# A new hand-written order for the first block, and a last product taken by output tile, in a kernel of attention and two MLPs on one core

## The chip, the cores and the metric

The kernel runs on one core of one Trainium2 chip. The metric is the device time of one execution in microseconds (us), and the comparison is with the kernel before the change. The engines that the text names are TensorE (PE, with its weight loads as PEld), VectorE (DVE), ScalarE (ACT), GpSimd (POOL) and the queue of SyncE (SP) that issues most of the DMA transfers.

## What is computed

A chunked attention with eight memory keys is followed by two MLPs over its 3072 rows of 512 numbers. The scale factors of the inputs are left out here.

```python
# q, k, v: 4 batches x 8 heads x 768 x 64; mem_k, mem_v: 4 x 8 x 8 x 64; chunk 32
for c in range(24):
    q_c = q[:, :, 32*c : 32*c + 32]
    k_ctx, v_ctx = k, v of rows max(0, 32*c - 16) .. min(768, 32*c + 40)
    scores = q_c @ concat(mem_k, k_ctx).T / 8
    a = exp(scores - max(scores)); a = a / (sum(a) + 1e-9)
    out[:, :, 32*c : 32*c + 32] = a @ concat(mem_v, v_ctx)
x = out as 3072 rows x 512
h = max(max(x @ w1, x @ w2), x @ w3)        # 512 -> 768
x = h @ w_mid                               # 768 -> 512
h = x @ w_in                                # 512 -> 2048
g = 0 where h <= -1, (h + 1)**2 / 4 between, h where h >= 1
out = g @ w_out                             # 2048 -> 512
```

## The kernel before

**Products.** Each of the four MLP stages keeps its operands as a sum of two rounded numbers, a high and a low part. `mm3` (L544) issues three matmuls for each product: high by high (L545), high by low (L546) and low by high (L547). The weights of the first MLP arrive in chunks of 512 KB (the steps `f`, L124 and L126). Two chunks make a pair, and a pair q is turned into its high and low part in six steps: `wa` (ACT, L139), `wr` (ACT, L143), `wc` (DVE, L147, L148 and L150), `wd` (DVE, L155), `wh` (ACT, L204, the high part) and `ws` (DVE, L209, the low part).

**Blocks.** Rows are taken in blocks of 512, which are four units of 128 rows. Attention is computed unit by unit: loads of k, q and v (`lk`, `lq`, `vs`; `vs` is two transfers of 56 KB), transposes of k and q (`tk` L297, `tq` L328), their copies (`ck`, `ek`, `kw`, `cq`), scores (`s`, L402), the maximum (`mx`, DVE L415 and L416), the exponential (`ex`, ACT L419), the division (`n`, DVE L422, L423 and L425), transposes of the probabilities (`a`, L444), their copy (`ca`), the product with v (`o`, L470), and the high and low part of its result (`cx`, ACT L481, and `dx`, DVE L485).

**The first block.** For block 0 nothing runs ahead that could cover the loads, so the order of its work and of units 0 to 8 is written by hand, as the string `PLAN` (L42 to L58). Its words are the steps above with their number, and the program issues them from left to right. Each engine and the SP queue takes its instructions in this order and waits at its head. A transfer that SP issues also waits for the one eight places ahead of it. `g0` to `g2` are the first products (with w1, w2, w3) over the left 256 of the block's 512 rows, which need units 0 and 1; `l0` to `l2` are the same for the right 256 rows, which need units 2 and 3. From `l3` on a product covers all 512 rows. `gt` and `lt` take the maximum of the three (ACT copy or DVE L582), `lh` splits it, `m` is a product with w_mid. The words `d3` and `d7` are `warm` (L1057): four matmuls of 256 columns on a constant, whose result in bank 3 or 7 nobody reads. A group of them into a bank whose content is still to be read waits for the reader; a group behind `o3` into bank 3 waits for `dx3`.

**The rest.** Behind the plan a list of slots goes through the other blocks and then through the second MLP, in three pairs of blocks. Its last part, `pair_l4`, runs 48 steps for a pair. In each step `l4_mms` (L764) issues three matmuls into the accumulator of each of two output tiles d. At the very end `last_evict` (L930) goes through two halves of 256 rows: DVE adds for both tiles (L937), PE transposes (L939), ACT copies the half (L941) and SP sends it (L943, 256 KB).

Of the kernel before, what the change touches and what calls it, by code (L numbers as in the profile page):

```python
# [39 lines left out]


PLAN = """  # L42
d7 lk1 lmem0 d3 d7 tk1 ck1 mem0 d3 lk0 tk0 lq0 ck0 d3 f0 d3 tq0 d3 ek1 f1 d3 kw0 cq0 wa0 lk2 lm0 s0
lq1 lk3 mx0 lq2 d7 vs0 tk2 vs6 ck2 lk4 d3 wc0 ex0 d3 ek2 tq1 cq1 kw1 wr0 n0 d3 d3 tk3 ck3 f3 d3 s1
ek3 tq2 kw2 d3 d3 d3 mx1 vs5 wd0 ex1 d3 a0 d3 cq2 ca0 s2 wh0 d7 d7 f2 n1 wa1 d7 vs2 lq3 d3 d7 a1 vs1
mx2 d3 mv0 vs3 ex2 lq4 tk4 d7 d3 d7 wr1 ck4 d3 ws0 ek4 tq3 wc1 wd1 kw3 vs7 lk5 mv1 vs4 d3 o0 cq3 f5
f4 cx0 n2 ca1 s3 d7 tq4 wh1 tk5 ck5 mx3 mv2 d3 d3 a2 cq4 dx0 ex3 vs8 d7 vs10 o1 ek5 kw4 d3 ws1 n3
lq5 s4 cx1 wa2 dx1 ca2 vs9 mx4 vs11 wc2 kw5 g0 ex4 d3 vs13 f7 g1 vs12 gt0 gt1 tq5 a3 d7 n4 cq5 vs15
s5 vs14 f6 wr2 wd2 o2 cx2 ca3 f9 vs16 dx2 g2 a4 gt2 wh2 f8 o3 mx5 d7 vs19 ws2 cx3 dx3 ex5 d3 n5 l0
wa3 d3 wr3 lt0 vs18 wc3 vs17 wa4 l1 lt1 l2 wd3 lt2 wr4 ca4 wc4 lq7 l3 f11 lt3 wh3 f10 a5 l4 wd4 o4  # L50
tq7 lh2 wh4 ws3 l5 ws4 wa5 cq7 lk6 cx4 f13 lt4 wc5 l6 d3 f12 wr5 wd5 ca5 lq6 vs23 vs20 lt5 wa6 tk6
lt6 lk7 dx4 wh5 wr6 vs21 vs22 ck6 wc6 tq6 f14 ws5 lk8 l7 tk7 wd6 lh5 lm1 ck7 f15 lt7 ek7 o5 kw6 wh6
cq6 lq8 vs25 cx5 l8 wa7 wr7 ws6 f17 dx5 f16 tk8 s6 l9 mv6 mx6 lt8 lt9 wc7 ck8 m0 wd7 vs27 l10 ek8
wa8 lk9 wc8 f19 ex6 f18 tq8 tk9 wh7 m1 wr8 ws7 wd8 lh8 lt10 kw7 wh8 f21 f20 l11 ws8 ck9 n6 wa9 m2 a6
vs24 wr9 wa10 lk11 lt11 wc9 vs26 wd9 wr10 f23 ca6 l12 l13 cq8 o6 wh9 wc10 ws9 wd10 lt12 s7 lh11 lt13
l14 mx7 cx6 wh10 l15 dx6 f22 vs28 m3 ex7 f24 lt14 f25 ek9 n7 ws10 wa11 vs29 lq9 wc11 wr11 vs30 a7
l16 lt15 kw8 ca7 lh14 vs31 lt16 o7 wd11 cx7 dx7 l17 s8 wh11 lt17 mx8 ws11 ex8 lq10 lh17 lk10
""".split()  # L58
# [10 lines left out]
def attention_then_two_mlps(ctx, tc, q, k, v, mem_k, mem_v, w1, w2, w3, w_mid, w_in, w_out, out):  # L69
    nc = tc.nc  # L70
# [856 lines left out]

    extra, acc4 = [], {}

    def last_evict(p):  # L930

        for i in range(2):
            z = banks[i].rearrange("p (t c) -> p t c", t=2)
            c = slice(i * HK, (i + 1) * HK)
            for d in range(2):
                u2 = fb[4 + d]
                nc.vector.tensor_tensor(out=u2[:, c], in0=acc4[5][d][:, c], in1=u2[:, c], op=ALU.add)  # L937
                for t in range(2):
                    nc.tensor.transpose(z[:, t, d * P:(d + 1) * P], u2[:, (2 * i + t) * P:(2 * i + t + 1) * P], ident)  # L939
            o = fb[i].rearrange("p (t c) -> p t c", t=2)  # L940
            nc.scalar.copy(out=o, in_=z)  # L941
            r0 = 2 * p * TB + 2 * i * P
            nc.sync.dma_start(out=out[r0:r0 + 2 * P, HK:].rearrange("(t p) d -> p t d", p=P), in_=o)  # L943
# [299 lines left out]
```

## Time and profile before

| what | us |
|---|---|
| median of three runs (lowest, highest) | 950.63 (950.12, 950.81) |
| the profiled execution | 953.2 |
| its span in the profile | 951.4 |
| PE busy | 941.1 (99%) |
| DVE busy | 706.7 (74%) |
| ACT busy | 569.5 (60%) |
| POOL busy | 339.3 (36%) |
| DMA share of 16 engines | 53.5% |

PE is at work nearly all the time, in 7154 matmuls. The span is divided by the profile into 40 slices. PE shows 90% or more in all of them but the first and the last, and the row of the granted clock shows 9 in all but one. So the time that is not PE work at full rate lies in the first slices and in the last one, and a reader has to open these two places.

### The profile page before, as it was taken

The page shows a single profiled execution, that of the slowest core. Times are in us where ns is not written, and L with a number is a line of the kernel's source. Part 1 is how long each engine was busy: PE and PEld are TensorE (multiplying, and loading weights), DVE is VectorE, ACT ScalarE, POOL GpSimd, SP SyncE. Part 2 cuts the span into 40 slices and gives each one's busy share as a digit, 9 for nine tenths or more (in the row PEclk, how much of TensorE's full clock was granted, in tenths as well). Part 3 has the DMA queues.
Part 4 walks back from the last instruction along what each step waited for, and adds up shares of the span by engine and source line. Part 5 has one row for each costly group of instructions (what it writes and reads, how often), then busy time and mean ns, then how long its engine had stood idle before and what let it go on. Part 6 is the DMA issues. An engine that isn't in the chain of part 4 may idle for free.

```text
span 951.4 us, 18968 instructions
## 1 busy us (share of the span) xinstructions
PE 941.1 (99%) x7154; PEld 777.7 (82%) x7154; DVE 706.7 (74%) x995; ACT 569.5 (60%) x1037; POOL 339.3 (36%) x331
## 2 busy tenths in 40 slices
PE   8999999999999999999999999999999999999998
PEld 6888888888888888888888888888888888888886
DVE  5989866687887878743347778987777998778854
ACT  6667546554553444333357777677777776777763
POOL 0000002321321111112656654555665555655542
PEclk9989999999999999999999999999999999999999
DMA  9877647677757686433423339524236744233823
GB/s 218 204 197 220 166 115 188 172 232 198 206 155 190 184 199 205 145 110 112 138 84 99 95 97 291 155 39 122 84 91 205 213 112 106 81 91 90 260 67 67
DMA packets 245549, 142.84 MB, mean 150 GB/s; under 512 B 174290, under 2 KB 223186, under 8 KB 245458
## 3 DMA queue, kind: packets, MB, share of 16 engines
q1 hardware_dynamic: 245458, 141.63, 53.5%
q8 instruction: 56, 0.92, 0.4%
q14 instruction: 35, 0.29, 0.1%
HBM read 109.87 MB, written 31.46 MB: 149 GB/s over the span
## 4 chain that ended last, share of the span: by engine, by line
PE 95%; DMA 2%; DVE 1%; SPq 1%; issue 0%; ACT 0%; DVEq 0%
PE psums L545 30%; PE psums L547 30%; PE psums L546 30%; PE psums L463 2%; PE psums L402 2%; DMA kq<-in_k_dram 1%; DMA st<-in_moe_w_dram 1%; PE psums L470 1%; DMA vw<-in_v_dram 1%; PE psums L297 1%; SPq L289 0%; PE psums L1061 0%; PE psums L328 0%; DVE c L155 0%; DVE p L425 0%
## 5 line engine op out<-in xcount | busy, mean ns | idle before, releaser
L545 PE MATMUL psums<-xh,hi 128*128 128x512 f32 (+1 forms) x444 | 173.8, 391 | 0.0
L546 PE MATMUL psums<-xl,hi 128*128 128x512 f32 (+1 forms) x444 | 171.0, 385 | 0.5 <-DVE xl L485 0.5
L564 POOL TENSOR_TENSOR hl_a<-t,hh_a 128x512 fp32r<-128x512 f32 x30 | 40.3, 1343 | 367.4 <-ACT hh_a L562 367.4
L547 PE MATMUL psums<-xh,lo 128*128 128x512 f32 (+1 forms) x444 | 171.0, 385 | 0.0
L858 POOL TENSOR_TENSOR hb<-h,hb 128x512 fp32r<-128x512 f32 x72 | 99.4, 1381 | 92.6 <-PE psums L547 59.9
L850 ACT CAST hb<-h 128x512 fp32r<-128x512 f32 x144 | 88.8, 622 | 48.2 <-PE psums L546 46.5
L582 DVE TENSOR_TENSOR t<-psums,t 128x512 f32<-128x512 f32 (+1 forms) x74 | 49.8, 673 | 71.4 <-PE psums L547 69.4
L545 PEld LDWEIGHTS psums<-xh,hi 128*128 128x128 f32 x444 | 84.1, 189 | 17.2
L546 PEld LDWEIGHTS psums<-xl,hi 128*128 128x128 f32 x444 | 84.2, 190 | 16.5 <-DVE xl L485 0.7
L547 PEld LDWEIGHTS psums<-xh,lo 128*128 128x128 f32 x444 | 84.0, 189 | 16.6
L677 POOL TENSOR_TENSOR hb<-ra,hb 128x256 fp32r<-128x256 f32 x96 | 75.2, 796 | 59.1 <-ACT hb L676 55.9
L742 ACT ACTIVATE psums<-h 128x512 f32<-128x512 f32 x96 | 57.9, 603 | 60.1 <-DVE h L828 24.0
L547 PE MATMUL psums<-t,hb 128*128 128x512 f32 x192 | 74.8, 390 | 0.0
L545 PE MATMUL psums<-t,hb 128*128 128x512 f32 x192 | 74.7, 389 | 0.0
L546 PE MATMUL psums<-t,hb 128*128 128x512 f32 x192 | 74.7, 389 | 0.0
L677 POOL TENSOR_TENSOR hb<-rb,hb 128x256 fp32r<-128x256 f32 x72 | 55.4, 776 | 39.2 <-ACT hb L676 39.2
L856 DVE TENSOR_TENSOR hb<-psums,hb 128x512 fp32r<-128x512 f32 x66 | 44.9, 680 | 24.8 <-PE psums L547 20.1
L743 ACT ACTIVATE psums<-psums 128x512 f32<-128x512 f32 x96 | 55.9, 582 | 3.1
L545 PE MATMUL psums<-hh_a,hi 128*128 128x512 f32 x144 | 57.3, 398 | 0.0
L883 DVE TENSOR_TENSOR h<-h,h 128x1024 f32<-128x1024 f32 (+1 forms) x42 | 56.5, 1368 | 0.0
L547 PE MATMUL psums<-hh_a,lo 128*128 128x512 f32 x144 | 56.2, 390 | 0.0
L546 PE MATMUL psums<-hl_a,hi 128*128 128x512 f32 x144 | 56.1, 389 | 0.0
(151 smaller groups left out, 2269.0 us busy)
## 6 DMA issues: line engine op xcount, KB each, us to landing
ra<-cd SPq DMA_DIRECT2D x24, 512.0 KB
st<-in_moe_w_out_dram SPq DMA_DIRECT2D x22, 512.0 KB
t<-sd SPq DMA_DIRECT2D x21, 512.0 KB
st<-in_moe_w_dram SPq DMA_DIRECT2D x18, 512.0 KB
st<-in_moe_w_in_dram SPq DMA_DIRECT2D x16, 512.0 KB
sd<-st SPq DMA_DIRECT2D x8, 896.0 KB
vw<-in_v_dram SPq DMA_DIRECT2D x59, 112.0 KB
h<-yd SPq DMA_DIRECT2D x12, 512.0 KB
```

Of the source, the lines that this page charges most:

```text
L545: nc.tensor.matmul(out, whi, xhi, start=first, stop=False)
L546: nc.tensor.matmul(out, whi, xlo, start=False, stop=False)
L547: nc.tensor.matmul(out, wlo, xhi, start=False, stop=last)
L564: e.tensor_tensor(out=lo, in0=h, in1=hi.bitcast(F32), op=ALU.subtract)
L582: nc.vector.tensor_tensor(out=t, in0=s, in1=t, op=ALU.max)
L677: nc.gpsimd.tensor_tensor(out=c[:, 1], in0=t, in1=c[:, 0].bitcast(F32), op=ALU.subtract)
L742: nc.scalar.activation(out=a, in_=x, func=AF.Relu, bias=0.5, scale=0.5)
L743: nc.scalar.activation(out=a, in_=a, func=AF.Square)
L850: nc.scalar.copy(out=hi, in_=x)
L856: nc.vector.tensor_tensor(out=lo, in0=y, in1=hi.bitcast(F32), op=ALU.subtract)
L858: nc.gpsimd.tensor_tensor(out=lo, in0=x, in1=hi.bitcast(F32), op=ALU.subtract)
L883: nc.vector.tensor_tensor(out=x, in0=y, in1=z, op=op)
```

## The change

There are two edits.

1. `PLAN` has the same steps in another order, and four more dummy groups (two `d3` and two `d7`): 45 where there were 41.
2. The last two steps of the last pair's product with w_out are held back and done by output tile: both steps for d = 0, then both for d = 1. `last_evict` is called twice. Behind the first tile DVE adds its 512 rows. Behind the second tile PE transposes the first tile, ACT copies it and SP sends it in one transfer (256 KB, in pieces of 512 bytes); then DVE adds the second tile in two halves, PE transposes each, DVE copies the first half (SP sends it, 128 KB) and ACT copies the second half and sends it on its own queue (128 KB).

```diff
 PLAN = """
...
-s5 vs14 f6 wr2 wd2 o2 cx2 ca3 f9 vs16 dx2 g2 a4 gt2 wh2 f8 o3 mx5 d7 vs19 ws2 cx3 dx3 ex5 d3 n5 l0
...
+d3 o1 d7 n3 s4 cx1 d7 ca2 dx1 mx4 vs10 vs13 wa2 wc2 vs12 vs15 d3 lq5 wr2 ex4 vs14 a3 f6 g0 g1 o2 f7
+wd2 gt0 cx2 f8 gt1 wh2 dx2 g2 tq5 ca3 n4 gt2 o3 ws2 kw5 cq5 cx3 wa3 wr3 f9 vs16 dx3 d3 a4 s5 l0 d3
...
-    def l4_mms(acc, w, hi, lo, f):
-        for d in range(2):
+    def l4_mms(acc, w, hi, lo, f, half=range(2)):
+        for d in half:
             r = slice(d * P, (d + 1) * P)
             mm3(acc[d], w[:, 0, r], w[:, 1, r], hi, lo, f == 0, f == HF - 1)
-        hb.extend((hi, lo))
+        if 0 in half:
+            hb.extend((hi, lo))
...
-    def last_evict(p):
+    def last_evict(p, last):
...
+        r0 = 2 * p * TB
+        rows = out[r0:r0 + TB, HK:].rearrange("(t p) d -> p t d", p=P)
+
+        def turn(d, t):
+            nc.tensor.transpose(banks[d][:, t * P:(t + 1) * P], fb[4 + d][:, t * P:(t + 1) * P], ident)
+
+        both_halves = [slice(i * HK, (i + 1) * HK) for i in range(2)]
+
+        def add(d, c):
+            u2 = fb[4 + d][:, c]
+            nc.vector.tensor_tensor(out=u2, in0=acc4[5][d][:, c], in1=u2, op=ALU.add)
+
+        if not last:
+            add(0, slice(0, TB))
+            return
+        for t in range(4):
+            turn(0, t)
+        nc.scalar.copy(out=fb[0], in_=banks[0])
+        nc.sync.dma_start(out=rows[:, :, 0:P], in_=fb[0].rearrange("p (t d) -> p t d", d=P))
+        for i, c in enumerate(both_halves):
+            add(1, c)
+            for t in (2 * i, 2 * i + 1):
+                turn(1, t)
+        for i, c in enumerate(both_halves):
+            (nc.scalar.copy if i else nc.vector.tensor_copy)(out=fb[1][:, c], in_=banks[1][:, c])
+            (nc.scalar if i else nc.sync).dma_start(
+                out=rows[:, 2 * i:2 * i + 2, P:], in_=fb[1][:, c].rearrange("p (t d) -> p t d", d=P))
...
+            if last and i >= len(FACTORS) * HF - 2:
+                late.append((w, hi, lo, f))
+                if len(late) == 2:
+                    for d in range(2):
+                        for x in late:
+                            l4_mms(acc4[k], *x, [d])
+                        last_evict(p, d)
+                continue
             l4_mms(acc4[k], w, hi, lo, f)
```

In the changed kernel the lines below the plan stand one further on (L289 is L290), the dummies are L1085, and the new end is L938 to L959.

**The loads ahead of the last rows of v.** The SP queue before, from the load of q for unit 5 (`lq5` is the second of these rows' `kq`) to the first chunk behind it; `vw` and `vxl` are rows of v, `st` are weight chunks:

```order
L289 DMA vxl<-in_v_dram 56x4x64 x4
L246 DMA kq<-in_q_dram 128x8x64
L289 DMA vxl<-in_v_dram 56x4x64 x4
L289 DMA vw<-in_v_dram 56x4x64 x2
L124 DMA st_710<-in_moe_w_out_dram 128x1024
L289 DMA vw<-in_v_dram 56x4x64 x6
L126 DMA st_710<-in_moe_w_dram 128x4x256
L126 DMA st_821<-in_moe_w_dram 128x4x256
```

The same stretch of the SP queue in the changed kernel:

```order
L290 DMA vxl<-in_v_dram 56x4x64 x8
L290 DMA vw<-in_v_dram 56x4x64 x6
L247 DMA kq<-in_q_dram 128x8x64
L290 DMA vw<-in_v_dram 56x4x64 x2
L127 DMA st_724<-in_moe_w_dram 128x4x256
L125 DMA st_724<-in_moe_w_out_dram 128x1024
L127 DMA st_787<-in_moe_w_dram 128x4x256 x2
```

The chunk `st_710` of 512 KB (f7) stood ahead of the last three pairs of transfers that `o3` needs, and now all chunks from f6 on stand behind them. Up to the last row of v the queue holds otherwise the same loads.

**PE between `o3` and `l0`.** Before, from the last group of `o3` (`vw`) over two dummy groups to the first product of the right half (`xh_510`, `xl_511`, `hi_382`, `lo_383`):

```order
L470 MATMUL psums<-aT_819,vw 64x32 x18
L1061 LDWEIGHTS ident
L1061 MATMUL psums<-ident 128x256 [waits DVE_49]
...
L1061 MATMUL psums<-ident 128x256 [waits DVE_49]
...
L545 MATMUL psums<-xh_510,hi_382 128x256 [waits Activation_49]
L546 MATMUL psums<-xl_511,hi_382 128x256
L547 MATMUL psums<-xh_510,lo_383 128x256
```

The same stretch of PE in the changed kernel, with the transposes of q for unit 5 ahead of it:

```order
L329 MATMUL psums<-ident,kq 128x128 x3
...
L471 MATMUL psums<-aT_810,vw 64x32 x18
L1085 LDWEIGHTS ident
L1085 MATMUL psums<-ident 128x256 [waits DVE_49]
...
L445 MATMUL psums<-ident,p_814 128x128 x4
L403 MATMUL psums<-kw,qTb_86 32x64 [waits Activation_49]
L403 MATMUL psums<-kw,qTb_86 32x64 x31
L546 MATMUL psums<-xh_524,hi_322 128x256 [waits Activation_49]
```

One dummy group is gone from this place, and the transposes of unit 4's probabilities (`a4`) and the scores of unit 5 (`s5`, 64 matmuls), which stood ahead of `o3`, now stand between the group that waits for `dx3` and `l0`.

**DVE behind `dx3`.** Before, from the low part of x (`xl_511`) to the low part of weight pair 3 (`lo_979`), which `l5` reads; `c_911` is pair 3 and `c_926` pair 4:

```order
L485 TENSOR_TENSOR xl_511<-psums,xh_510 128x4x128
L422 TENSOR_REDUCE few<-ex_eps 128x8
L423 RECIPROCAL few<-few 128x8
L425 TENSOR_TENSOR p_897<-ex_eps,few 128x512
L147 TENSOR_SCALAR c_911<-c_911 128x1024
...
L155 ISA c_926<-st_821,c_926 128x2048
L564 TENSOR_TENSOR hl_a_0_1038<-t_0_726,hh_a_0_1037 128x512
L209 TENSOR_TENSOR lo_979<-c_911,hi_978 128x1024
```

In the changed kernel the low part of pair 3 is `lo_987` (`c_853` is pair 3, `c_943` pair 4):

```order
L486 TENSOR_TENSOR xl_525<-psums,xh_524 128x4x128
L411 MEMSET psums 32x2x4x8
L416 TENSOR_REDUCE few<-psums 128x8
L417 TENSOR_TENSOR ex_eps<-psums,few 128x8x64
L148 TENSOR_SCALAR c_853<-c_853 128x1024
...
L156 ISA c_943<-st_787,c_943 128x2048
L210 TENSOR_TENSOR lo_987<-c_853,hi_986 128x1024
```

The maximum of unit 5 (`mx5`), which stood ahead of `dx3`, now stands behind it and waits for `s5`; the division of unit 5 moved behind the low part.

## Rows read from the trace of the kernel before

**Rows 1.** Windows: us, busy of PE, PEld, DVE, ACT, POOL, granted clock, DMA share, GB/s.

```profile
9.70:13.10 3.40, 1.88 (x63) 1.45 (x43) 2.16 (x4) 1.18 (x2) 0.00 (x0) 1.00 1.06 210
43.80:47.20 3.40, 1.92 (x52) 1.59 (x53) 3.11 (x5) 1.00 (x2) 0.00 (x0) 1.00 0.86 261
47.20:54.00 6.80, 6.33 (x61) 5.35 (x55) 4.73 (x8) 4.09 (x6) 0.00 (x0) 0.50 0.93 216
54.00:945.50 891.50, 891.47 (x6228) 736.15 (x6227) 665.97 (x926) 533.51 (x978) 338.38 (x322) 1.00 0.52 147
...
55.00:100.00 45.00, 45.00 (x404) 37.50 (x404) 41.47 (x51) 31.82 (x46) 0.00 (x0) 1.00 0.76 203
```

**Rows 2.** Chain that ended last, around the last rows of v: start, us, what.

```profile
41.66 4.89 DMA vw<-in_v_dram
...
48.12 0.59 ACT xh L481
```

**Rows 3.** Timeline of the SP queue: start, us, line, transfer, count.

```profile
39.40 0.36 SPq L124 DMA_DIRECT2D st<-in_moe_w_out_dram  x1
39.81 2.73 SPq L289 DMA_DIRECT2D vw<-in_v_dram  x6
```

**Rows 4.** Timeline of PE: start, us, line, operation, count, idle time before.

```profile
20.60 0.86 PE L402 MATMUL psums<-kw,qTb 64*32 64x64 f32 x64
...
23.59 0.60 PE L444 MATMUL psums<-ident,p 128*128 128x128 f32 x4
24.02 0.60 PE L1061 MATMUL psums<-ident 128*128 128x256 bf16 x4
24.46 0.60 PE L297 MATMUL psums<-ident,kq 128*128 128x128 f32 x4
...
46.59 1.45 PE L470 MATMUL psums<-aT,vw 64*64 64x32 f32 x48 [1.48 <-DMA vw<-in_v_dram]
47.98 1.04 PE L1061 MATMUL psums<-ident 128*128 128x256 bf16 x4
49.48 1.01 PE L1061 MATMUL psums<-ident 128*128 128x256 bf16 x4 [0.47 <-DVE xl L485]
50.15 0.56 PE L545 MATMUL psums<-xh,hi 128*128 128x256 f32 x1
50.51 0.41 PE L546 MATMUL psums<-xl,hi 128*128 128x256 f32 x1
50.72 0.41 PE L547 MATMUL psums<-xh,lo 128*128 128x256 f32 x1
...
54.11 0.28 PE L547 MATMUL psums<-xh,lo 128*128 128x256 f32 x1
54.23 0.28 PE L545 MATMUL psums<-xh,hi 128*128 128x256 f32 x1
```

**Rows 5.** Timelines of DVE and PE up to the low part of weight pair 3.

```profile
45.40 0.69 DVE L416 TENSOR_TENSOR ex_eps<-psums,few 128x512 f32<-128x512 f32 x1
...
50.91 0.69 DVE L147 TENSOR_SCALAR c<-c 128x1024 f32<-128x1024 f32 x1
...
55.58 0.42 DVE L582 TENSOR_TENSOR t<-psums,t 128x256 f32<-128x256 f32 x1 [1.99 <-ACT st L143]
...
62.39 2.35 DVE L209 TENSOR_TENSOR lo<-c,hi 128x1024 fp32r<-128x1024 f32 x2
...
64.80 0.39 PE L547 MATMUL psums<-xh,lo 128*128 128x512 f32 x1
```

**Rows 6.** Timeline of all engines behind the last product.

```profile
945.47 0.39 PE L547 MATMUL psums<-hb,b 128*128 128x512 f32 x1
...
945.90 1.09 DVE L937 TENSOR_TENSOR f<-psums,f 128x256 f32<-128x256 f32 x3 [0.26 <-PE psums L547]
946.38 1.10 PE L939 MATMUL psums<-ident,f 128*128 128x128 f32 x6 [0.24 <-DVE f L937]
946.86 1.25 ACT L941 COPY f<-psums 128x512 f32<-128x512 f32 x2 [6.82 <-PE psums L939]
```

More of the change, by code (lines that the diff above doesn't have):

```diff
@@ L42 @@
 PLAN = """
[L43 to L47, printed above, removed]
@@ L48 @@
-lq5 s4 cx1 wa2 dx1 ca2 vs9 mx4 vs11 wc2 kw5 g0 ex4 d3 vs13 f7 g1 vs12 gt0 gt1 tq5 a3 d7 n4 cq5 vs15
-s5 vs14 f6 wr2 wd2 o2 cx2 ca3 f9 vs16 dx2 g2 a4 gt2 wh2 f8 o3 mx5 d7 vs19 ws2 cx3 dx3 ex5 d3 n5 l0
-wa3 d3 wr3 lt0 vs18 wc3 vs17 wa4 l1 lt1 l2 wd3 lt2 wr4 ca4 wc4 lq7 l3 f11 lt3 wh3 f10 a5 l4 wd4 o4
-tq7 lh2 wh4 ws3 l5 ws4 wa5 cq7 lk6 cx4 f13 lt4 wc5 l6 d3 f12 wr5 wd5 ca5 lq6 vs23 vs20 lt5 wa6 tk6
-lt6 lk7 dx4 wh5 wr6 vs21 vs22 ck6 wc6 tq6 f14 ws5 lk8 l7 tk7 wd6 lh5 lm1 ck7 f15 lt7 ek7 o5 kw6 wh6
@@ L53 @@
[L53 to L57, printed above, removed]
+d3 d7 d3 lk0 d3 tk0 d3 lk1 f0 ck0 tk1 lmem0 lm0 f1 lq0 lk2 d3 ck1 lq1 mem0 wa0 d7 d3 d7 ek1 d7 d3
@@ new lines @@
+kw0 d7 lk3 tq0 cq0 d3 tk2 ck2 mv0 ek2 wc0 s0 tq1 wr0 cq1 d3 mx0 tk3 d3 d3 ex0 wd0 d7 kw1 d7 ck3 vs0
+vs2 s1 lk4 wh0 ek3 n0 kw2 vs7 d7 lq2 a0 f2 f3 d7 mx1 d3 tq2 ex1 vs4 lq3 cq2 vs3 tk4 d3 ws0 s2 n1 ck4
+ek4 mx2 vs1 wa1 mv2 d3 d7 d3 d7 d3 d3 wr1 lk5 wc1 d7 lq4 d3 ca0 wd1 tq3 d3 kw3 ex2 a1 mv1 n2 cq3 d3
+wh1 o0 cx0 vs6 s3 d7 tk5 vs5 dx0 mx3 ca1 d3 ck5 f5 f4 a2 ek5 vs9 vs8 kw4 ws1 ex3 vs11 tq4 d3 cq4 d3
+d3 o1 d7 n3 s4 cx1 d7 ca2 dx1 mx4 vs10 vs13 wa2 wc2 vs12 vs15 d3 lq5 wr2 ex4 vs14 a3 f6 g0 g1 o2 f7
@@ new lines @@
+wd2 gt0 cx2 f8 gt1 wh2 dx2 g2 tq5 ca3 n4 gt2 o3 ws2 kw5 cq5 cx3 wa3 wr3 f9 vs16 dx3 d3 a4 s5 l0 d3
+l1 lt0 lq6 vs19 vs17 lk6 ca4 mx5 wc3 wa4 lt1 wd3 l2 ex5 lt2 l3 wr4 l4 wh3 wc4 wd4 ws3 n5 tq6 vs18
+f11 lt3 tk6 ck6 wh4 f10 lt4 l5 f13 f12 cq6 ws4 lh2 lt5 wa5 o4 l6 wr5 lk7 cx4 wa6 wr6 wc5 dx4 d3 a5
+vs23 wd5 lh5 lm1 lq7 wc6 wd6 ca5 l7 vs22 vs20 lt6 f14 vs21 tk7 d3 d3 tq7 wh5 f15 ck7 ek7 m0 kw6 f17
+cq7 ws5 wh6 lt7 lk8 s6 wa7 o5 f16 mx6 cx5 ws6 dx5 wr7 m1 lq8 wa8 wc7 l8 tk8 lk9 wr8 wd7 l9 lt8 ex6
@@ L58 @@
+l10 vs24 tq8 wc8 lh8 wd8 ck8 wh7 f19 ws7 f18 tk9 vs25 lt9 lq10 wh8 f20 m2 ek8 l11 kw7 lt10 wr9 wa9
+ck9 vs27 n6 ws8 vs26 f21 a6 wc9 lt11 cq8 l12 wd9 ca6 wa10 mv6 wh9 o6 wc10 cx6 ws9 s7 wr10 lt12 l13
+lt13 lh11 dx6 lq9 mx7 vs29 ex7 l14 wd10 l15 vs30 wh10 n7 f22 m3 ek9 vs31 a7 kw8 lt14 f23 wa11 ws10
+ca7 lt15 l16 wr11 f24 wc11 vs28 lh14 o7 cx7 l17 lt16 dx7 s8 wd11 lt17 mx8 wh11 f25 lh17 ex8 ws11
+lk10 lk11
 """.split()
@@ L928, in attention_then_two_mlps @@
     extra, acc4 = [], {}
-    def last_evict(p):
[L932 to L943, printed above, removed]
+    def last_evict(p, last):
[22 more added lines that the diff above has]
+                out=rows[:, 2 * i:2 * i + 2, P:], in_=fb[1][:, c].rearrange("p (t d) -> p t d", d=P))
     def pair_l4(p, steps):
         last = p + 1 == NB // 2
+        late = []
         for i in range(len(FACTORS) * HF):
@@ L979, in pair_l4 @@
                     prep(p + 1, name)
-        if last:
-            last_evict(p)
-        else:
+        if not last:
             for f in range(2):
```

## The prediction, made before the changed kernel ran

> **What bounds the kernel now.** First the windows, for where PE is not at work at full rate [rows 1]. From 54.0 to 945.5 PE is busy 891.47 of 891.50 us at a granted clock of 1.00. Nothing in that long stretch can be gained by an order that starts the same matmuls, and the change leaves those matmuls alone, except the last twelve. So the change is worth what it does before 54.0, what it does to the unbroken row just behind (where PE has no idle time, so each added matmul counts in full), and what it does behind 945.5.
>
> Then the chain of waits around the first product of the right half [rows 2]. The last rows of v are issued at 41.66 and land 4.89 us later; `o3` follows, and at 48.12 ACT's high part. PE's own row says the same [rows 4]: 1.48 us of waiting for v, 48 of the 64 matmuls of `o3` from 46.59, a dummy group, another one that waits for DVE's low part (`dx3`), and `l0` at 50.15. From the end of `o3`'s matmuls (47.98) to the group that waits for the low part (49.48) are 1.5 us that no order of PE's work shortens.
>
> Then the clock [rows 1, 4]. [...] It fell behind a stretch in which PE was busy 1.92 of 3.40 us with no dummy group in it. At the lower level a product matmul of 256 columns takes 0.21 us (50.51 to 50.72) and at the higher 0.12 (54.11 to 54.23), a ratio of 0.56. Of the 3.85 us from 50.15 to 54.0 the lower level thus costs 3.85 x 0.44 = 1.7 us.
>
> Last the end [rows 6]: the last product matmul starts at 945.47, three DVE adds run 945.90 to 946.99, the second ACT copy ends at 948.11, and the span ends at 951.4.
>
> **The change, part by part.** All terms are differences against the profiled execution (953.2, span 951.4). I add their sum to the median, 950.63: the profiled one is 2.6 us longer as a whole, and no term is a share of the span.
>
> *The load of v.* The chunk f7 (512 KB) leaves the place ahead of the last three pairs of v. The core moved 216 to 261 GB/s in these stretches [rows 1], so 512 KB are 2.0 to 2.4 us. The least is the time of one issue, if the queue and not the bytes is what v waits for: 39.40 to 39.81, 0.4 us [rows 3]. The most is some 3.4: the DMA share ahead of 47.2 is 0.86 [rows 1], and the last seven us without such gaps would be 1.0 us shorter. I take 2.2, because the queues are nearly full. PE can use it: it gives up `a4` (0.43) and `s5` (0.79, 64 matmuls from 20.60 to 21.39) ahead of `o3`, and gets three dummy groups there more at 0.44 each (24.02 to 24.46) [rows 4]. These are 1.2 against 1.3, so it reaches its wait for v at about 45.1 (46.59 less 1.48) as before, or earlier, if some of the groups lie in waits. The matmuls of `o3` then end at 45.8 instead of 47.98, and the dummy group that waits for `dx3` starts at 47.3.
>
> *`a4` and `s5` behind `dx3`.* They are now queued behind that group, and `l0` behind them: 0.44 + 0.43 + 0.79 = 1.66 us at full rate. `l0` would start at 48.95, 1.2 us earlier than 50.15.
>
> *The clock.* The stretch before the fall has much the same content as now: the last product of the left half, one set of transposes (`tq5` where `a4` was), `o3` in pieces, no dummy group, and now 1.5 us without any work between `o3` and the group. A row speaks for no fall: from 9.70 to 13.10 PE was busy only 1.88 of 3.40 us and the clock stayed [rows 1]. I take the fall at the same place, since the stretch is nearest to the one that had it. Then the group, `a4` and `s5` run at the lower level, at the ratio above 2.8 us instead of 1.66, and `l0` starts at 50.1, as before. But PE now works on without a pause from 47.3. Before, the last pause ended at 49.48 [rows 4] and the rate was back at 54.0, 4.5 us later; that gives 51.8 here. The other end is a return as `l0` starts. I take 51.0: `l0` pays 0.9 x 0.44 = 0.4 instead of 1.7, a gain of 1.3.
>
> [...]
>
> *Dummy groups in the unbroken row.* Behind `l0` stand four groups instead of two. PE has no cover there: 2 x 0.44 = +0.9.
>
> *Waits in the unbroken row.* `l5` needs the low part of weight pair 3 from DVE. Before, DVE begins this pair at 50.91 and ends its low part at 63.6 (62.39 and half of two operations of 2.35), with 1.99 us of idle time on the way; PE reads it at 64.80 [rows 5]. Now `mx5` (two operations of 0.7) stands behind `dx3` and waits for `s5`, so DVE begins the pair at 50.1 + 1.4 = 51.5; `hl`, of the same size (0.7), and the division move behind. Without the idle time the same steps take 12.7 - 2.0 - 0.7 = 10.0 us, to 61.5. PE would read it at 64.80 less the 1.3 from above and less 1.0 of attention work that moved behind `l5` (`o4`, the transposes `a5` and `tq7`, for two sets of transposes): 62.5. That is room of 1.0 us and no wait. `o5` has a new wait for a DVE memset. I put +0.2 on both together, between 0 and 1.
>
> *The end.* The twelve matmuls are the same, so the last ends at the same place. Behind it DVE has two adds of 256 columns instead of three, 0.36 us less, and PE two pairs of transposes less. The first tile's copy and its transfer run ahead of the last copies. Against it stand two copies in a row (DVE then ACT, of 256 columns each) where one copy of 512 columns (0.6) ended the chain, and a transfer that ACT issues, of which the trace has none. The last transfer is 128 KB instead of 256. I take -0.3, between -0.7 (shorter adds and half the bytes) and +0.3 (a slower issue, pieces of 512 bytes).
>
> Sum: 0.0 (`l0` starts as before) - 1.3 + 0.9 + 0.2 - 0.3 = -0.5. The forecast is 950.63 - 0.5 = 950.1.
>
> **The rivals.**
>
> *No fall of the clock.* `l0` starts at 48.95 (-1.2) and the lower level's 1.7 is saved whole: -1.2 - 1.7 + 0.9 + 0.2 - 0.3 = -2.1, so 948.5. For it speaks the stretch from 9.70; against it that this stretch held dummy groups, which the new one does not. It hardly gets better than this: DVE would have the low part at 60.4, and PE read it at 60.9.
>
> *The fall as long as before.* The rate returns at 54.0: `l0` starts at 50.1 and pays the same 1.7: 0.0 + 0.9 + 0.2 - 0.3 = +0.8, so 951.4. For it: PE has again 1.5 us without work just behind the fall. Against it: after 47.3 there is none.
>
> *Slower: PE waits for the weight rounding.* From 55 to 100 DVE is busy 41.47 of 45.00 us while PE has no pause at all [rows 1], so what DVE loses there beyond its room PE loses too. It decides from the point where DVE idles over 1.0 us between `s5` and the low part of pair 3, and it idled 1.99 before, released by ACT. With three waits of that length, 6.0, of which the 1.0 and the idle time of before (1.99) cost nothing, PE loses 3.0: -0.5 - 0.2 + 3.0 = +2.3, so 952.9. For it: PE comes 2.3 us earlier to the same steps, and f6 and f7 now both land behind v. Against it: the room above.
>
> *The transfers don't come earlier.* v gains only the 0.4 us of an issue. `o3` ends at 47.6, the group starts at 49.1, and at the lower level `l0` at 51.9 (+1.75); back at 54.0, it pays 0.9 instead of 1.7 (-0.8): +1.75 - 0.8 + 0.9 + 0.2 - 0.3 = +1.75, so 952.4.
>
> **How the numbers follow.** The forecast has 0.40, no fall 0.28, the long fall 0.12, the wait for weights 0.11, transfers as before 0.09. The last two are slower than before, the third too by less than can be told. A measurement of this kernel tells a change from none at about 0.2%, 1.9 us: below 948.7 is faster, above 952.5 slower. No fall lies around the first bound; with a part of the forecast whose v comes early and whose end gains more, I give faster 0.27, slower 0.11 (most of the wait for weights, and nearly half of the transfers as before), and 0.62 to no change. The range reaches from 947.6 (no fall, v 3.0 us early, the end at its best end for half) to 952.4 (the transfers as before).
>
> **What would show it.** In the trace after: the last v lands at about 44.4 and the group behind `o3` starts at 47.3; the granted clock falls near 47.2 and returns near 51; `l0` starts at 50.1; the row from there to the end has no idle time over 0.2 us, and four dummy groups; the second copy behind the last product ends 0.2 to 0.4 us earlier than now against the last matmul. I am wrong if the clock stays at 1.00, if idle time with DVE as its end stands ahead of `l5` or `l8`, or if PE reaches `o3` later than v does.

## The result, and the profile after

The changed kernel took 957.36 us (median of 5 runs, 956.25 to 960.21), the kernel before 950.81 beside it (950.12 to 952.0). The ratio is 1.0067, with a 95% interval of 1.005 to 1.0084: slower by 6.4 us, where 0.5 us less was forecast and 952.4 was the end of the range.

The profiled execution took 957.36 us, its span is 954.9. Its windows, with the columns of [rows 1], the second from `l3` (the first product over all 512 rows) to the last product matmul:

```profile
47.20:54.00 6.80, 5.35 (x141) 4.96 (x142) 4.12 (x7) 3.90 (x6) 0.00 (x0) 1.00 1.02 287
56.09:949.18 893.09, 890.13 (x6214) 734.03 (x6212) 666.00 (x928) 532.38 (x976) 341.38 (x322) 1.00 0.52 147
```

Two things are to be seen. The granted clock did not fall here: it was 1.00 where it was 0.50 before [rows 1]. And the row behind `l0`, in which PE had no pause before, now has 893.09 - 890.13 = 2.96 us of them. What ended them, in the view of waits on PE from 47 on (us in total, times, longest):

```profile
PE psums L1085 <- DVE xl L486: 2.3, 2, 1.4
PE psums L403 <- ACT xh L482: 1.4, 1, 1.4
PE psums L471 <- DMA vw<-in_v_dram: 0.7, 1, 0.7
PE psums L471 <- DVE psums L409: 0.4, 1, 0.4
PE psums L547 <- DVE hb L858: 0.3, 1, 0.3
```

PE around `o3` and `l0`, to be laid beside [rows 4]:

```profile
45.86 0.53 PE L471 MATMUL psums<-aT,vw 64*64 64x32 f32 x18
47.14 0.90 PE L471 MATMUL psums<-aT,vw 64*64 64x32 f32 x46 [0.75 <-DMA vw<-in_v_dram]
49.48 0.60 PE L1085 MATMUL psums<-ident 128*128 128x256 bf16 x4 [1.45 <-DVE xl L486]
49.92 0.60 PE L445 MATMUL psums<-ident,p 128*128 128x128 f32 x4
50.45 0.86 PE L403 MATMUL psums<-kw,qTb 64*32 64x64 f32 x64
51.24 0.39 PE L546 MATMUL psums<-xh,hi 128*128 128x256 f32 x1
```

The last rows of v are waited for until 47.14, later than 46.59 before. The group that waits for `dx3` starts at 49.48, to the hundredth as before, and `a4` and `s5` behind it put `l0` at 51.24.

Where the three waits in the row behind `l0` come from, first on PE, then what stood ahead on DVE and on ACT:

```profile
70.19 0.60 PE L1085 MATMUL psums<-ident 128*128 128x256 bf16 x4 [0.82 <-DVE xl L486]
...
79.66 0.55 PE L471 MATMUL psums<-aT,vw 64*64 64x32 f32 x24 [0.38 <-DVE psums L409]
...
104.42 0.86 PE L403 MATMUL psums<-kw,qTb 64*32 64x64 f32 x64 [1.45 <-ACT xh L482]
...
68.31 1.23 DVE L151 SCALAR_TENSOR_TENSOR c<-st,c 128x1024 uint32<-128x1024 uint32 x1
69.45 0.69 DVE L486 TENSOR_TENSOR xl<-psums,xh 128x512 fp32r<-128x512 f32 x1
...
101.79 1.16 ACT L140 ACTIVATE c<-st 128x1024 f32<-128x1024 f32 x1 [2.01 <-DMA kq<-in_q_dram]
102.86 1.03 ACT L205 CAST hi<-c 128x1024 fp32r<-128x1024 f32 x1
103.79 0.57 ACT L482 CAST xh<-psums 128x512 fp32r<-128x512 f32 x1
```

The dummy group behind `l6` waits for `dx4`, which DVE does only behind the three operations on a weight pair. The scores `s7` wait for `cx6`, the high part of unit 6 in the same pair of banks, and `cx6` stands on ACT behind `wa10` and `wh9`; ACT had been without work for 2.01 us, until a transfer landed. The product `o5` waits for the memset of `s6` on DVE, in the pair of banks that both use since `m0` moved ahead of them. The last line of the table of waits lies far behind the plan, at 621.7 us, in the second MLP: a product there waits for a low part on DVE.

### The profile page after: what moved, and what is told of

Same layout as the page of the kernel before. It is cut to its first block, busy times and chain, and to the rows that moved or that the text cites. A ratio compares the mean times of both kernels' runs of the same rounds, so it can differ in the third digit from the quotient of the medians.

```text
span 954.9 us, 18991 instructions
## 1 busy us (share of the span) xinstructions
PE 941.5 (99%) x7170; PEld 777.1 (81%) x7170; DVE 705.9 (74%) x995; ACT 570.0 (60%) x1037; POOL 342.3 (36%) x331
## 4 chain that ended last, share of the span: by engine, by line
PE 92%; DMA 3%; SPq 2%; DVE 1%; ACT 1%; issue 0%; DVEq 0%; ACTq 0%
PE psums L546 29%; PE psums L547 29%; PE psums L548 29%; PE psums L464 2%; PE psums L403 2%; DMA st<-in_moe_w_dram 1%; SPq L290 1%; DMA kq<-in_k_dram 1%; PE psums L1085 1%; DMA vw<-in_v_dram 0%; PE psums L471 0%; PE psums L329 0%; DMA kq<-in_q_dram 0%; SPq L127 0%; DVE c L151 0%
## 5 line engine op out<-in xcount | busy, mean ns | idle before, releaser
L860 POOL TENSOR_TENSOR hb<-h,hb 128x512 fp32r<-128x512 f32 x72 | 102.3, 1422 | 90.3 <-PE psums L548 60.7
L547 PE MATMUL psums<-hl_a,hi 128*128 128x512 f32 x144 | 56.1, 390 | 0.0
```

## The experiments

The first four runs part the two edits, and work from loads.

**The plan alone: `e1_plan_alone`.** The old end, with the new `PLAN`:

```diff
 PLAN = """
-d7 lk1 lmem0 d3 d7 tk1 ck1 mem0 d3 lk0 tk0 lq0 ck0 d3 f0 d3 tq0 d3 ek1 f1 d3 kw0 cq0 wa0 lk2 lm0 s0
...
+d3 d7 d3 lk0 d3 tk0 d3 lk1 f0 ck0 tk1 lmem0 lm0 f1 lq0 lk2 d3 ck1 lq1 mem0 wa0 d7 d3 d7 ek1 d7 d3
...
```

> The new PLAN with the old end. Theory PLAN: all that was lost is the plan's (PE waits in the row behind l0, 2.9 us in the profile, the two dummy groups, 0.9, and l0 later than before without a fall of the clock, 1 to 2), and the new end gains 0.2 to 0.3: about 957.4 to 957.7 against 950.8 of before. Rival END: the new end costs part of it (the transfer issued by ACT, pieces of 512 bytes): clearly below 957, down to 954.5 if the end cost 2.5.

Measured: 958.84 us (958.58 to 959.64) against 950.88, a ratio of 1.007 (1.0044 to 1.0096). The loss is the plan's; the ratio of both edits together, 1.0067, lies inside the interval. In this execution the clock did fall, and as long as before; the second window is again the one from `l3` on:

```profile
47.50:54.30 6.80, 5.37 (x140) 4.64 (x133) 1.72 (x4) 3.24 (x4) 0.00 (x0) 0.50 1.06 317
58.66:951.00 892.34, 890.03 (x6213) 734.28 (x6212) 664.58 (x928) 532.61 (x976) 341.04 (x322) 1.00 0.52 146
```

PE's timeline of the same run around it, at the lower level (0.50):

```profile
46.69 0.66 PE L329 MATMUL psums<-ident,kq 128*128 128x128 f32 x4 [1.69 <-DMA kq<-in_q_dram]
47.27 1.77 PE L471 MATMUL psums<-aT,vw 64*64 64x32 f32 x64
50.48 1.01 PE L1062 MATMUL psums<-ident 128*128 128x256 bf16 x4 [1.44 <-DVE xl L486]
51.28 1.06 PE L445 MATMUL psums<-ident,p 128*128 128x128 f32 x4
52.27 1.03 PE L403 MATMUL psums<-kw,qTb 64*32 64x64 f32 x53
```

The group, `a4` and `s5` take 2.9 us here (50.48 to `l0` at 53.38) and 1.76 in the changed kernel's own trace at full rate. The transposes `tq5` wait 1.69 us for their load, `lq5`, and PE stands ahead of `o3` meanwhile: in the new plan `lq5` is issued behind `vs15`.

**The end alone: `e2_end_alone`.** The new end, with the old `PLAN` (the second half of the diff in front, nothing else):

```diff
-        if last:
-            last_evict(p)
-        else:
+        if not last:
             for f in range(2):
                 evict(p, 5, f)
```

> The old PLAN with the new end. Theory PLAN: 0.2 to 0.3 us faster than before (950.5), the time from the last product matmul to the end of the span 5.7 us instead of 5.95. Rival END: up to 2.5 us slower (953.3). The trace has the old plan once more: if the clock doesn't fall at 47 in it, the profile of before showed a state that its median run does not have.

Measured: 951.92 us (950.75 to 952.94), a ratio of 1.0006 (0.9991 to 1.0021): no difference in the time. In the traces the stretch from the last product matmul to the end of the span is 5.7 to 5.8 us in all kernels with the new end (950.1 - 944.32 here) and 5.9 to 6.0 with the old one. So the end gains 0.2 us, too little for the time to show. The run is also a second trace of the old plan. Its windows:

```profile
47.20:54.00 6.80, 5.34 (x83) 4.87 (x84) 5.54 (x9) 3.76 (x6) 0.00 (x0) 1.00 1.01 239
55.59:944.32 888.73, 888.70 (x6205) 733.40 (x6204) 665.42 (x925) 532.33 (x977) 338.39 (x322) 1.00 0.53 147
```

And on PE's timeline the wait for v, 1.31 us where [rows 4] have 1.48:

```profile
47.73 1.23 PE L470 MATMUL psums<-aT,vw 64*64 64x32 f32 x48 [1.31 <-DMA vw<-in_v_dram]
```

With the same plan as before, and a wait for v nearly as long, the clock stayed at 1.00. The fall that my sum was built on is in one of these two executions and not in the other. From `l3` to the last product matmul this run takes 888.73 us, as the profile of before does (56.74 to 945.47). The changed kernel takes 4.36 more.

**New order of work, old order of loads, and the other way round: `e3_new_work_old_loads`, `e4_old_work_new_loads`.** The words that load, in the order of one plan, stand in the places of the other plan's loads. The first lines of the two plans:

```diff
+d3 d7 d3 lk1 d3 lmem0 lk0 tk0 d3 ck0 tk1 lq0 f0 f1 lk2 lm0 d3 ck1 lq1 mem0 wa0 d7 d3 d7 ek1 d7 d3
...
+d7 lk0 lk1 d3 d7 tk1 ck1 f0 lmem0 mem0 d3 tk0 ck0 d3 lm0 d3 f1 lq0 tq0 d3 ek1 d3 kw0 cq0 wa0 lk2 s0
...
```

> All work and dummies in the order of the new PLAN, the loads in the order of the old one (put into the places of the new loads), old end. Theory LOADS: what PE waits for in the row behind l0 comes from loads that land later under the new order, so those waits (2.9 us in the profile) go and 1 to 1.5 remain from the dummies: 951.5 to 953. Rival WORK: the order on DVE and ACT makes the waits, whatever the loads: 956 to 958.

> All work and dummies in the order of the old PLAN, the loads in the order of the new one, old end. Theory LOADS: slower than before by 3 to 5 us (954 to 956), with PE waiting behind l0. Rival WORK: within 1 us of before (950 to 952).

Measured: 969.02 us (1.0175, 1.0144 to 1.0207) and 972.35 us (1.0207, 1.0179 to 1.0235). Both theories fall: either mixture is far worse than either plan. On the same chip the new work loses 10 us by the old loads (969.02 against 958.84 of `e1`), and the old work 21 us by the new ones (972.35 against 950.88). In both one load of q comes late behind `l3`:

```profile
73.05 1.12 PE L329 MATMUL psums<-ident,kq 128*128 128x128 f32 x4 [5.92 <-DMA kq<-in_q_dram]
```

```profile
74.82 1.12 PE L328 MATMUL psums<-ident,kq 128*128 128x128 f32 x4 [7.09 <-DMA kq<-in_q_dram]
```

The first line is from the new work with old loads, the second from the other. The two orders of a plan are fitted to each other, so the question cannot be put as work against loads. The next runs take single words.

**Three edits to the new plan.** `e5_two_groups_less` drops two dummy groups, `e6_s7_ahead_of_cx6` moves one word, `e7_three_edits` has both, and also drops the group that waits for `dx4`:

```diff
-vs23 wd5 lh5 lm1 lq7 wc6 wd6 ca5 l7 vs22 vs20 lt6 f14 vs21 tk7 d3 d3 tq7 wh5 f15 ck7 ek7 m0 kw6 f17
+vs23 wd5 lh5 lm1 lq7 wc6 wd6 ca5 l7 vs22 vs20 lt6 f14 vs21 tk7 tq7 wh5 f15 ck7 ek7 m0 kw6 f17
...
-ck9 vs27 n6 ws8 vs26 f21 a6 wc9 lt11 cq8 l12 wd9 ca6 wa10 mv6 wh9 o6 wc10 cx6 ws9 s7 wr10 lt12 l13
+ck9 vs27 n6 ws8 vs26 f21 a6 wc9 lt11 cq8 l12 wd9 ca6 wa10 mv6 wh9 o6 s7 wc10 cx6 ws9 wr10 lt12 l13
...
-f11 lt3 tk6 ck6 wh4 f10 lt4 l5 f13 f12 cq6 ws4 lh2 lt5 wa5 o4 l6 wr5 lk7 cx4 wa6 wr6 wc5 dx4 d3 a5
+f11 lt3 tk6 ck6 wh4 f10 lt4 l5 f13 f12 cq6 ws4 lh2 lt5 wa5 o4 l6 wr5 lk7 cx4 wa6 wr6 wc5 dx4 a5
```

> The changed kernel without the two dummy groups behind tk7. Theory EACH COUNTS: PE does 0.88 us less in the row behind l0, 956.5 against 957.4 of the changed kernel. Rival SWALLOWED: the wait of s7 at 103 (1.45, for a high part on ACT that stands behind a weight chunk's landing) is set by transfers and grows by what PE gains: no change, 957.4, with 2.3 us of idle time there.

> The changed kernel with the scores s7 issued ahead of cx6, whose reading of the same pair of banks they wait for. Theory EACH COUNTS: the wait of 1.45 us goes, 955.9. Rival MOVED: the next thing that needs the chunk waits instead, less than 0.5 us gained (957).

> The changed kernel without the two dummy groups behind tk7, without the one behind l6 that waits for dx4, and with s7 ahead of cx6. Theory EACH COUNTS: 0.88 + 0.44 + 0.82 + 1.45 = 3.6 us less than the changed kernel, 953.8; the row from l3 to the last product matmul then takes 889.5 us instead of 893.1 (888.7 with the old plan). Rival SWALLOWED or MOVED: half of it or less, 955.5 and above, with new waits in that row.

These runs were on another chip, where before took 952.11 us, so I compare ratios: 1.0054 (1.0039 to 1.007), 1.005 (1.0037 to 1.0062) and 1.0024 (1.0012 to 1.0035), with 957.68, 957.5 and 954.86 us. Against the 1.0067 of the changed kernel the first two are 1.2 and 1.6 us less, inside the intervals; the third is 4.1 less, outside them (3.6 were expected). The window from `l3` to the last product matmul, of `e5`, `e6` and `e7` in this order:

```profile
57.49:949.74 892.25, 889.08 (x6206) 733.43 (x6204) 664.61 (x928) 532.89 (x976) 340.91 (x322) 1.00 0.52 146
```

```profile
54.79:946.48 891.69, 889.95 (x6214) 734.22 (x6212) 665.46 (x928) 533.89 (x977) 341.09 (x322) 1.00 0.52 147
```

```profile
58.44:947.18 888.74, 888.22 (x6202) 733.16 (x6201) 664.98 (x928) 532.29 (x976) 341.57 (x322) 1.00 0.52 147
```

893.09 became 892.25, 891.69 and 888.74. In `e5` PE's work is 1.05 us less (890.13 to 889.08), but its pauses are not: 892.25 - 889.08 = 3.17 us. The wait of `s7` is shorter there (0.7), and the one in the second MLP longer, 1.5 us instead of 0.3, so this run by itself does not put the rival out:

```profile
622.30 0.50 PE L547 MATMUL psums<-hb,t 128*128 128x512 f32 x1 [1.51 <-DVE hb L858]
```

With all three edits the row is back at the length of the old plan, 888.73, the wait in the second MLP is gone too, and the one pause left is the 0.5 us of `o5`. So it is shown that these edits bring back the 4.36 us of this row. The shares are read from the views: 0.88 of dummy groups, 2.96 of pauses (1.45 for `cx6`, 0.82 for `dx4`, 0.38 and 0.3 for the smaller ones), and some 0.5 by which PE was busy longer around them. What stays above before, 2.3 us, I put ahead of `l3`, since row and end are as long as in the old plan with the new end.

**`a4` and `s5` ahead of `o3` again: `e8_a4_s5_ahead_of_o3`.**

```diff
-wd2 gt0 cx2 f8 gt1 wh2 dx2 g2 tq5 ca3 n4 gt2 o3 ws2 kw5 cq5 cx3 wa3 wr3 f9 vs16 dx3 d3 a4 s5 l0 d3
+wd2 gt0 cx2 f8 gt1 wh2 dx2 g2 tq5 ca3 n4 gt2 kw5 cq5 a4 s5 o3 ws2 cx3 wa3 wr3 f9 vs16 dx3 d3 l0 d3
```

> The changed kernel with a4 and s5 back ahead of o3. Theory EACH COUNTS: of the 1.22 us that they take behind dx3, 0.8 go into the wait for v (0.84 us in the changed kernel), so l0 starts 0.8 earlier, at about 50.4, and the time is 956.5. Rival: the clock now falls as in the profile of before, since nothing but o3 and a dummy group lies between g2 and l0, and l0 pays 1.7: 958.

Measured: 958.32 us, 1.0064 (1.0041 to 1.0088), as the changed kernel. Inconclusive: in its trace `tq5` waited 1.61 us for `lq5`, `a4` and `s5` ran behind that and not in the wait for v, and the clock fell as well (0.21 us from one product matmul to the next behind `l0`, 53.40 to 53.61, where at 1.00 it is 0.12; the mean of the execution is 0.996).

**The load of q for unit 5 earlier: `e10_lq5_earlier`**, on top of the three edits (two lines of the plan are joined here):

```diff
-vs9 vs8 kw4 ws1 ex3 vs11 tq4 d3 cq4 d3 d3 o1 d7 n3 s4 cx1 d7 ca2 dx1 mx4 vs10 vs13 wa2 wc2 vs12 vs15 d3 lq5
+vs9 vs8 kw4 ws1 ex3 vs11 tq4 d3 cq4 d3 d3 o1 d7 n3 s4 cx1 d7 ca2 dx1 mx4 vs10 lq5 vs13 wa2 wc2 vs12 vs15 d3
```

> The kernel of three edits with the load of q for unit 5 (lq5) issued ahead of vs13, eight transfers earlier and nearer to its place in the old plan. Theory TQ5: the wait of the transposes tq5 for this load (1.4 to 1.7 us in three of six traces with the new plan, PE standing ahead of o3) is gone, and l0 starts at most 6.9 behind g2: 953.5 to 954.5 against 954.9. Rival: v now lands one transfer later and o3 waits for it instead: 954.9.

Measured: 953.02 us, 1.0018 (1.0008 to 1.0028) on a third chip, against 1.0024 without it. In the trace `tq5` does not wait, and neither does `o3`:

```profile
45.87 0.60 PE L328 MATMUL psums<-ident,kq 128*128 128x128 f32 x4
46.56 1.39 PE L470 MATMUL psums<-aT,vw 64*64 64x32 f32 x64
49.48 0.60 PE L1084 MATMUL psums<-ident 128*128 128x256 bf16 x4 [1.53 <-DVE xl L485]
49.91 0.87 PE L444 MATMUL psums<-ident,p 128*128 128x128 f32 x4
50.72 1.18 PE L402 MATMUL psums<-kw,qTb 64*32 64x64 f32 x64
51.83 0.58 PE L545 MATMUL psums<-xh,hi 128*128 128x256 f32 x1
```

But `l0` starts 7.5 us behind the start of `g2` (44.33), where the old plan has 6.8 (`e2`) and at most 6.9 was expected: the 1.5 us behind `o3` have no work in them, and `a4` and `s5` stand behind these. From 50.1 to 53.5 the granted clock was 0.50 in this execution, so the group, `a4` and `s5` took 2.35 us (49.48 to 51.83) instead of 1.76; without that 0.6 `l0` would start 6.9 us behind `g2`. Whether the two ratios differ can't be told. The row from `l3` to the last product matmul is 888.58 us here, a second trace in which the three edits bring it back.

**The first term of the prediction alone: `e9_f7_behind_v`.** One word of the old plan:

```diff
-lq5 s4 cx1 wa2 dx1 ca2 vs9 mx4 vs11 wc2 kw5 g0 ex4 d3 vs13 f7 g1 vs12 gt0 gt1 tq5 a3 d7 n4 cq5 vs15
-s5 vs14 f6 wr2 wd2 o2 cx2 ca3 f9 vs16 dx2 g2 a4 gt2 wh2 f8 o3 mx5 d7 vs19 ws2 cx3 dx3 ex5 d3 n5 l0
+lq5 s4 cx1 wa2 dx1 ca2 vs9 mx4 vs11 wc2 kw5 g0 ex4 d3 vs13 g1 vs12 gt0 gt1 tq5 a3 d7 n4 cq5 vs15
+s5 vs14 f7 f6 wr2 wd2 o2 cx2 ca3 f9 vs16 dx2 g2 a4 gt2 wh2 f8 o3 mx5 d7 vs19 ws2 cx3 dx3 ex5 d3 n5 l0
```

> The kernel before with one word of its PLAN moved: f7 (512 KB) behind vs14. It is the prediction's first term alone. Theory BYTES (the prediction): v lands 2.0 to 2.4 us earlier against g2, PE's wait in o3 (1.3 to 1.5) is gone, and l0 starts 1.3 to 2.2 earlier than the 6.8 to 7.5 us behind the start of g2 that the old plan shows: 949 to 950.5 against 951 to 952. Rival PLACES: v waits for its place behind eight transfers in flight, gains one place of some 0.5 us, and the wait in o3 shrinks by that only: within 0.5 us of before.

Measured: 952.21 us, 0.9998 (0.9986 to 1.001). The time is that of before, as the rival had it, and yet the mechanism of the first theory is there. PE around `o3`, and behind `l0`, with the copy on ACT that it waits for:

```profile
44.31 0.60 PE L444 MATMUL psums<-ident,p 128*128 128x128 f32 x4
44.84 1.14 PE L470 MATMUL psums<-aT,vw 64*64 64x32 f32 x64
45.91 0.61 PE L1061 MATMUL psums<-ident 128*128 128x256 bf16 x4
48.08 0.60 PE L1061 MATMUL psums<-ident 128*128 128x256 bf16 x4 [1.55 <-DVE xl L485]
48.43 0.36 PE L545 MATMUL psums<-xh,hi 128*128 128x256 f32 x1
...
57.05 0.66 PE L444 MATMUL psums<-ident,p 128*128 128x128 f32 x4 [0.76 <-ACT aT L448]
...
54.38 1.12 ACT L139 ACTIVATE c<-st 128x1024 f32<-128x1024 f32 x1 [2.89 <-DVE c L155]
55.40 1.14 ACT L143 ACTIVATE st<-st 128x1024 uint32<-128x1024 uint32 x1
56.43 0.56 ACT L448 COPY aT<-psums 128x512 f32<-128x512 f32 x1
```

`o3` runs without a wait, and `l0` starts 5.65 us behind `g2` (42.78) instead of 6.8 to 7.5. Behind it `a5` waits 0.76 us for `ca4`, which stands on ACT behind `wa4` and `wr4`, and the stretch from `l3` to the last product matmul is 889.84 us (53.27 to 943.11) instead of 888.73. Of the 1.2 us gained 1.1 are given back.

**The old plan without its two dummy groups behind `l0`, with the new end: `e11_old_two_groups_less`.**

```diff
-wa3 d3 wr3 lt0 vs18 wc3 vs17 wa4 l1 lt1 l2 wd3 lt2 wr4 ca4 wc4 lq7 l3 f11 lt3 wh3 f10 a5 l4 wd4 o4
-tq7 lh2 wh4 ws3 l5 ws4 wa5 cq7 lk6 cx4 f13 lt4 wc5 l6 d3 f12 wr5 wd5 ca5 lq6 vs23 vs20 lt5 wa6 tk6
+wa3 wr3 lt0 vs18 wc3 vs17 wa4 l1 lt1 l2 wd3 lt2 wr4 ca4 wc4 lq7 l3 f11 lt3 wh3 f10 a5 l4 wd4 o4
+tq7 lh2 wh4 ws3 l5 ws4 wa5 cq7 lk6 cx4 f13 lt4 wc5 l6 f12 wr5 wd5 ca5 lq6 vs23 vs20 lt5 wa6 tk6
```

> The old PLAN with the new end and without its two dummy groups behind l0 (the one between l0 and l1 and the one behind l6). Theory EACH COUNTS: 0.88 us less in PE's row than the old plan and 0.2 less at the end: 950.0 where before is 951, and the row from l3 to the last product matmul takes 888.3 instead of 888.7. Rival SWALLOWED: DVE's roundings set the row and PE waits by as much: no change.

Measured: 950.46 us against 951.76, 0.9985 (0.9974 to 0.9996): 1.4 us faster than before, where 1.1 were expected. The row is 888.32 us long and has no pause.

```profile
55.46:943.78 888.32, 888.30 (x6202) 733.20 (x6200) 665.80 (x925) 532.90 (x977) 338.32 (x322) 1.00 0.53 147
```

**Both, with `ca4` ahead of `wa4`: `e12_old_plan_three_words`.**

```diff
-wa3 wr3 lt0 vs18 wc3 vs17 wa4 l1 lt1 l2 wd3 lt2 wr4 ca4 wc4 lq7 l3 f11 lt3 wh3 f10 a5 l4 wd4 o4
+wa3 wr3 lt0 ca4 vs18 wc3 vs17 wa4 l1 lt1 l2 wd3 lt2 wr4 wc4 lq7 l3 f11 lt3 wh3 f10 a5 l4 wd4 o4
```

> The old PLAN with the new end, without the two dummy groups behind l0, with f7 behind vs14, and with ca4 (the copy on ACT that a5 waited for, 0.76 us, in the run with f7 moved alone) ahead of wa4. Theory GIVEN BACK (the earlier v is worth its 1.2 us where nothing behind l0 waits): l0 starts 5.6 to 5.8 behind the start of g2 instead of 6.7, the row from l3 to the last product matmul keeps 888.3, and the time is 1.2 us under the run without the two groups: a ratio to before of 0.997. Rival TIGHT: the weight chunks now land later, DVE and ACT wait for them, and PE waits at another place behind l0 for what v gained: 0.9985, as without the move.

Measured: 950.8 us against 951.63, 0.9986 (0.9977 to 0.9996). It beats before as the last one does, and by no more: the first theory's 0.997 lies outside the interval, the rival's 0.9985 inside. `a5` no longer waits, `l0` starts 5.63 us behind `g2` (44.31 to 49.94), as hoped, and 0.65 of the 1.1 us are lost again in the row (888.94 instead of 888.3), 0.4 of them in a wait for a load of q. The window from `l3` on, and the line of the waits on PE:

```profile
54.32:943.26 888.94, 888.50 (x6201) 733.25 (x6200) 666.02 (x925) 533.59 (x977) 338.45 (x322) 1.00 0.53 148
```

```profile
PE psums L328 <- DMA kq<-in_q_dram: 0.4, 1, 0.4
```

The remaining half microsecond is below what the runs can tell.

## Why the prediction was wrong, point by point

The step that failed by most is the +0.2 for waits in the row behind `l0`: the changed kernel has 2.96 us of them. The next is the gain of 1.3 from the clock, which the median of before did not hold. The third is the load of v, whose 2.2 us came only in part.

**The trace it was made against.** The sum took 1.7 us for the lower clock out of the profile of before, put 1.3 of them down as a gain, and took that from the median. But the profiled execution took 953.2 us, the three runs of the median 950.12 to 950.81, and the trace of `e2` has the same plan and no fall. The profile of before, with its 6.8 us at the lower level, has a mean granted clock of 0.996. In the later comparisons 19 of 99 runs of kernels with the old order of loads (before, `e2`, `e11`) have 0.997 or less, and 34 of 52 with the new plan (the changed kernel, `e1`, `e5` to `e8`, `e10`). The 17 such runs of the kernel before took 953.5 us in the mean, its 40 runs at 0.999 or more 951.4. So the gain was for the most part not in the baseline, and the new plan runs at the lower level more often, not less. Where in an execution it does so the mean does not tell. The trace of `e10`, with 0.996 too, has two stretches of 3.4 us, and the first is far ahead of `o3` (columns of [rows 1]):

```profile
22.80:26.20 3.40, 3.40 (x76) 2.42 (x75) 0.67 (x1) 2.45 (x5) 0.00 (x0) 0.50 1.11 236
50.10:53.50 3.40, 3.40 (x76) 2.90 (x75) 1.44 (x4) 2.18 (x2) 0.00 (x0) 0.50 1.02 325
```

**The length of the fall.** It was to end near 51, by PE's work without a pause: an estimate of mine, and no run showed such an end. In `e1`, `e5` and `e7` the granted clock is 0.50 for 6.8 us, as in [rows 1] (47.50 to 54.30 in the first two, 48.50 to 55.30 in `e7`), and `e8` has the same mean, 0.996; in `e10` it is 0.50 for 3.4 us around `l0`. The rival of the long fall named the price rightly in kind: the group, `a4` and `s5` at the lower level took 2.9 us in `e1` (2.8 by the sum). Traces with the fall have `l3` at 57.4 to 58.8 under the new plan and at 56.74 before; traces without it at 54.8 and 56.1 against 55.6. More of PE's work stands in the fall under the new plan, so it may cost more there. Between runs at 0.997 or less and runs at 0.999 or more lie 2.1 us for the kernel before and 2.1 to 3.1 for the kernels with the new plan, too few runs to tell.

**The load of v (-2.2).** By itself the mechanism was right: `e9` takes the wait for v away and moves `l0` by 1.2 us or more. In the changed kernel less of it came. In `e2` PE comes to its wait for v at 46.4, as in the changed kernel (45.86 and 0.53), and not at 45.1 as in the profile of before. There the wait ends at 47.73, here at 47.14, and the group that waits for `dx3` starts 0.9 us earlier (50.40 and 49.48). The end of the wait differs as much between executions: 46.59, 47.73 and 48.11 under the old order of loads (before, `e2`, `e11`), 46.05, 46.67 and 47.14 under the new one (`e5`, `e7`, the changed kernel). And `lq5` (256 KB) now stands among the last rows of v: where v was early enough, PE stood at `tq5`, 1.4 to 1.7 us in three traces (`e1`, `e6`, `e8`); in `e10`, where `lq5` stands earlier, PE waits for neither. The step that failed here is that I took the rest of the queue to be as before because it holds the same loads.

**`a4` and `s5` behind `dx3`.** The term itself was right (1.66 by the sum, 1.76 measured from 49.48 to 51.24). With an unchanged start of the group it is a loss and not a part of a gain: at the same clock `l3` starts 0.5 us later than in `e2` (56.09 against 55.59). That is one pair of executions; in `e6`, also without a fall, `l3` starts at 54.79.

**Dummy groups (+0.9).** Right: without two of them PE's work in the row is 1.05 us less (`e5`), and without the one that the old plan has there 0.40 less (888.70 to 888.30, `e2` and `e11`).

**Waits in the row behind `l0` (+0.2, at most 1).** This is the term that was most mis-sized: 2.96 us. I followed the one consumer that had the least room, the low part of pair 3, and that one did not wait: PE has no pause from `l0` up to the group behind `l6`. The three in the plan that did wait could be read from the order, but had no row before. The group behind `l6` was counted as 0.44 us of work, though it had been moved behind `dx4`; before, it stood ahead of that. `s7` had been moved behind `cx6`. `o5` I named and priced at next to nothing; it waited 0.38 to 0.5 us. The slower rival, DVE's rounding of weights, has the sum (3.0 us) by luck: its waits were for weights, and no product waited for one. The wait for `dx4` comes nearest to it, since DVE does three operations on a weight pair first. The wait in the second MLP (0.3) is in no trace of the old plan; where it comes from I didn't follow.

**The end (-0.3).** Right in kind, 0.2 in the traces and nothing to be told in the time.

**The row from 9.70 as a sign of no fall.** The changed kernel's trace has the new stretch with `tq5` and `a4` and no fall (1.00 from 47.20 to 54.00), `e1` the same order of work and a fall (0.50 from 47.50 to 54.30). So my reading of that row doesn't decide it; the executions differ.

Together: in the profiled execution 4.4 us in the row behind `l3` and 0.5 ahead of it make the 4.8 between its span, 954.9, and that of `e2`, 950.1, which has the same end. That is shown by `e7` for the row. In time the two are 5.5 us apart (957.36 and 951.87), since 0.7 more lie outside the span of the first. The last 1.0 or so is by how much `e2`'s execution lies above the median of before (950.81); that is not parted further. More frequent falls are not what makes the 6.4: the profiled execution, which has none, is the median of the five, and three of the five have a mean clock of 0.999. They are part of what `e7` keeps above before: at 0.999 or more its two runs took 953.2 us and the ten of before beside them 951.8. What makes an execution have the fall stays open. With f7 behind v, where `o3` does not wait, 1 of 22 runs has a mean clock of 0.997 or less (`e9`, `e12`), which speaks for the wait in `o3`; but `e10` has a fall from 50.1 on without that wait, and no run changes that wait alone.

## What to carry to other kernels

Where a change moves a step, look up every wait that its new place gives it, also for steps that only fill time: here a dummy waited 0.82 us for the `dx4` that now stood ahead of it, a product 0.38 for a memset in the pair of banks that both use, and the scores `s7` 1.45 for the copy of `cx6` out of theirs. A gain at one place of an order that is tuned elsewhere can be given back at the next place that was timed for the old arrival, as 1.1 of 1.2 us were in `e9`; follow it on to the point where PE has room. And where the profiled execution is slower than the median, as by 2.6 us here, take a second trace of the kernel before, or the clocks of its runs, before a stretch at a lower clock is counted as a gain.
